# Parallel linear attention and channel MLP: inverse deviations by GpSimd's power, a one-step norm, and another order of loads and transposes in the opening

## The chip, the cores and the metric

One core of one Trainium2 chip runs the kernel. The metric is the device time of one execution in microseconds (us), and the time of a kernel is the median over its runs. Engines are named as the profile names them: PE is TensorE (PEld its weight loads), DVE is VectorE, ACT is ScalarE, POOL is GpSimd, SP is SyncE, which here issues nearly all DMAs.

## The reference

For one batch of S = 2048 rows of D = 640 numbers, with H = 32 heads of 20 and F = 1728 hidden units:

```python
xn = layernorm(x)                          # (x - m) / sqrt(v + 1e-5)
# A: linear attention with learned features
q, k, v = split_heads(xn @ wqkv)
pq, pk = q @ w_phi, k @ w_phi              # per head, 20x20
phi = concat(softmax(p), softmax(-p))      # for q and for k
o = phi_q (phi_k^T v) / (phi_q (phi_k^T 1) + 1e-6)
A = o @ wo
# B: channel MLP; it normalises xn a second time
y = layernorm(xn)
B = gelu(y @ w1 + b1) @ w2 + b2
out = x + A + B
```

Both norms need only the mean m and the variance v of a row of x. The second one is y = (x - m) / sqrt(v (1 + eps) + eps^2), with eps = 1e-5. The attention branch is computed from the same y, with a factor per row (`rs_all`) put back in the exponentials.

## The kernel before, in words

Every float32 operand of a matmul is split into a rounded part `hi` and a rest `lo`, both of a type that PE takes at full rate, and a product is three matmuls: hi by hi, hi by lo, lo by hi (`mm3`, lines 69 to 72). ACT writes `hi` (line 61) and DVE or POOL subtracts to get `lo` (line 64). The work is transposed: channels lie on partitions, and rows of x (tokens) on the free axis, in four blocks of 512 tokens. PE works through the MLP in groups of two chunks of 128 hidden units: a first product (640 channels into 128 units, 5 steps `kc`, 15 matmuls of 512 columns for a chunk), gelu and split of the result, and a second product back to 640 channels (5 output tiles `m`, 6 matmuls each). The order of every engine's instructions in this part is the order in which the program writes them (`manual_schedule`), and each engine takes its queue in order. After the MLP of blocks 0 and 1 come the attention and then the rest of the MLP.

The change is in the opening, which makes block 0's `y` from the rows of x themselves, while the later blocks get theirs from xT (x transposed, in DRAM). It runs so:

- SP loads four tiles of 128 rows (`xb`, tiles 0 to 3; `x0` in the program), the identity for the transposes, the four first chunks of w1 (`r1` of chunks 0 to 3), then tiles 4 to 7 (`x1`), the chunks of w2 (`r2`), block 0 of xT (the MLP's accumulator `acc`), all 320 KB a piece but the identity and xT.
- `stats` (lines 132 to 162) takes mean and variance of each tile on DVE (two `bn_stats`, one `bn_aggr`), scales them into `q`, has ACT take the square roots (line 151; this needs another function table than gelu), and improves the root by a Newton step with reciprocals on DVE, which leaves `ry` (for y) and, some steps later, `rs_all`.
- `centre` (line 166, ACT) subtracts the mean and `scale` (lines 170 and 172, ACT and DVE) multiplies by `ry`.
- `make_y0` (line 179) transposes two tiles on PE into three banks (channel groups c0 of one, c12 and c34 of two chunks of 128 channels), and splits each bank into y's `hi` and `lo`. It is called for tiles 0 and 1 (`y01`, the first half, 256 tokens) and for tiles 2 and 3 (`y23`).
- `half_first` (line 547) runs the first product of chunks 0 and 1 on a half: 30 matmuls of 256 columns. Its results stay in four banks, and their gelu and split (`zs`, four of them: two chunks by two halves) are written into PE's later work.
- PE fills the time before with 18 matmuls of zeros (line 582).
- Then `p10` starts: the first product of chunks 2 and 3 on all 512 tokens of block 0 (two tiles, 30 matmuls; the first of them is the L70 at 18.64 us in the profile), then the second product of chunks 0 and 1 (`p00`), which needs all four `zs`. Beside it runs `next_y` (line 655), which is stepped once per `kc` of the matmuls (a tick): it turns the means and `ry` of tiles 4 to 7 into a row by a small transpose on PE (line 202), copies it (line 204, DVE), sends it to DRAM from ACT's queue (line 207) and back as a broadcast, and makes block 1's `y` from xT with it (lines 681 to 687). The four `zs` are called in it too: the first on the fourth tick, before the row is sent, the others after.

Weights of later chunks are split as they land: `parts[c][0]` is the split of w1's chunk c (line 61 on ACT, line 64 on POOL).

Of the kernel before, what the change touches and what calls it, by code (L numbers as in the profile page):

```python
# [43 lines left out]
DEN_EPS = 1e-6  # L44

# [6 lines left out]
def tile_kernel(ctx: ExitStack, tc: tile.TileContext, x, xT, wkT, wqT, wv, wphi, wo, w1, b1, w2, b2,  # L52
# [30 lines left out]
    cp.tile([P, 56], F32, name="pad")  # L83
    nc.vector.memset(ones1, 1.0)
    nc.scalar.activation(rs_all[0:1, 0:1], ones1[:, 0:1], AF.Sqrt)
# [46 lines left out]
    def stats(ts, xp, xbs, turned=False, eng=nc.vector):  # L132
# [16 lines left out]
        sr = xp.tile([P, 2, n], F32, name="sr", bufs=2)  # L149
        rr = xp.tile([P, 2, n], F32, name="rr", bufs=2)  # L150
# [3 lines left out]
        if turned:  # L154
            nc.vector.scalar_tensor_tensor(sr, sr, -1.0, rr, op0=ALU.mult, op1=ALU.subtract)
        else:
            nc.vector.tensor_tensor(sr, sr, rr, op=ALU.add)
        nc.vector.reciprocal(ry[:, ts], sr[:, 1, :])
        yield
        ra = xp.tile([P, n], F32, name="ra", bufs=2)  # L160
        nc.vector.reciprocal(ra, sr[:, 0, :])
        nc.vector.tensor_tensor(rs_all[:, ts], sr[:, 1, :], ra, op=ALU.mult)

    def centre(t, xb):

        nc.scalar.activation(xb, xb, AF.Identity, bias=mv[:, t, 0:1], scale=-1.0)

    def scale(t, xb, act=False):
        if act:
            nc.scalar.activation(xb, xb, AF.Copy, scale=ry[:, t:t + 1])  # L170
        else:
            nc.vector.tensor_scalar_mul(xb, xb, ry[:, t:t + 1])

    def scale_pair(t):
        scale(t, x0[t])
        scale(t + 1, x0[t + 1][:, :3 * P], True)
        scale(t + 1, x0[t + 1][:, 3 * P:])

    def make_y0(half, xbs, ptile):

        cols = slice(half * 256, half * 256 + 256)
        for c0, n in ((0, 1), (1, 2), (3, 2)):
            ps = ptile()
            for c in range(n):
                for i in range(2):
                    nc.tensor.transpose(ps[:, c * 256 + i * P:c * 256 + (i + 1) * P],
                                        xbs[i][:, (c0 + c) * P:(c0 + c + 1) * P], idt)
            src = ps[:, :n * 256].rearrange("p (c t) -> p c t", c=n)
            cs = slice(c0, c0 + n)
            split(y[0][0][:, cs, cols], y[0][1][:, cs, cols], src)  # L190
            yield
# [27 lines left out]
    class Mlp:  # L219
# [67 lines left out]
        def gelu(self, g, j, pz, gt, hh, hl, out=False):  # L287
# [4 lines left out]
            nc.scalar.activation(gt, pz, AF.Gelu_apprx_tanh, bias=b1t[:, 2 * g + j:2 * g + j + 1])  # L292
            split(hh, hl, gt)

        def passes(self, g, b, ws, hid=None):
# [7 lines left out]
            for j, (w1h, w1l, w2h, w2l) in enumerate(todo):  # L303
# [6 lines left out]
                else:  # L310
# [7 lines left out]
                    nc.scalar.activation(gt[0:64, :], tm, AF.Gelu_apprx_tanh, bias=b1t[0:64, 13:14])  # L318
# [101 lines left out]
        def cross(self, g, bs, before, later):  # L420
# [39 lines left out]
            def gelu(z, i):  # L460
                nc.scalar.activation(z, z, AF.Gelu_apprx_tanh, bias=b1t[:, 2 * g + i:2 * g + i + 1])
# [73 lines left out]
    dmas[0] = mlp.fetch_parts(0, r0)  # L535
    dmas[0][0]()
    x0 += load_x(range(2, 4), xp)
    dmas[1] = mlp.fetch_parts(1, r0)
    dmas[1][0]()
# [7 lines left out]
    def half_first(half, *order):  # L547
# [3 lines left out]
        last = {op[0]: op for op in order}  # L551
        for op in order:
            j, wi, yi, kc = op
            nc.tensor.matmul(pz[j], wc[j][wi][:, kc, :], y[0][yi][:, kc, cols], start=(wi, yi, kc) == (0, 0, 0), stop=last[j] == op)  # L554
# [1118 lines left out]
```

## Time and profile before

| | |
|---|---|
| runs | 703.95, 704.29, 705.25 us; median 704.29 us |
| span of the profiled execution | 702.3 us |
| PE busy | 697.2 us, 99% |
| DVE, POOL, ACT busy | 525.0, 455.9, 365.1 us |
| first real matmul of the opening (L554) | 9.27 us |
| first matmul of full width (L70) | 18.64 us |

The span runs from the first to the last instruction of the profiled execution; the device time holds some 2 us around it. A line of the timeline gives start and duration in us, engine, line of the kernel, operation, what it writes and reads, the shape, and how many instructions of a kind in a row were merged. A line of the groups gives count, busy time and the mean of one in ns. In the queue of SP or ACT (SPq, ACTq) a DMA's line is its issue, not its transfer. A matmul's row starts when PE takes it; its end is modelled, so that matmuls overlap, and the distance of two starts is what one costs.

### The profile page before, as it was taken

The page shows a single profiled execution, that of the slowest core. Times are in us where ns is not written, and L with a number is a line of the kernel's source. Part 1 is how long each engine was busy: PE and PEld are TensorE (multiplying, and loading weights), DVE is VectorE, ACT ScalarE, POOL GpSimd, SP SyncE. Part 2 cuts the span into 40 slices and gives each one's busy share as a digit, 9 for nine tenths or more (in the row PEclk, how much of TensorE's full clock was granted, in tenths as well). Part 3 has the DMA queues.
Part 4 walks back from the last instruction along what each step waited for, and adds up shares of the span by engine and source line. Part 5 has one row for each costly group of instructions (what it writes and reads, how often), then busy time and mean ns, then how long its engine had stood idle before and what let it go on. Part 6 is the DMA issues. An engine that isn't in the chain of part 4 may idle for free.

```text
span 702.3 us, 9854 instructions
## 1 busy us (share of the span) xinstructions
PE 697.2 (99%) x3357; PEld 587.7 (84%) x3357; DVE 525.0 (75%) x856; ACT 365.1 (52%) x615; POOL 455.9 (65%) x388
## 2 busy tenths in 40 slices
PE   9999999999999999999999999999999999999998
PEld 7888888888888888888888888888888888888886
DVE  7868654977755788788888887848688687789783
ACT  6434643344334545454444546457676666659360
POOL 3711314576245997798787969558689997577930
PEclk9999999999999999999999999999999999999999
DMA  9834633485621227325500707884345648872222
GB/s 325 259 110 128 193 108 98 157 279 166 216 106 75 94 76 233 86 91 199 123 1 3 190 0 282 240 241 117 121 145 160 184 148 285 290 274 69 75 76 105
DMA packets 67465, 107.62 MB, mean 153 GB/s; under 512 B 7623, under 2 KB 31975, under 8 KB 65791
## 3 DMA queue, kind: packets, MB, share of 16 engines
q1 hardware_dynamic: 67110, 106.98, 47.7%
q8 instruction: 26, 0.43, 0.3%
q14 instruction: 25, 0.20, 0.1%
q10 hardware_dynamic: 304, 0.01, 0.0%
HBM read 72.42 MB, written 34.55 MB: 152 GB/s over the span
## 4 chain that ended last, share of the span: by engine, by line
PE 98%; DVE 1%; ACT 0%; issue 0%; POOL 0%; DVEq 0%; POOLq 0%
PE bank L910 29%; PE bank L70 19%; PE bank L72 19%; PE bank L71 19%; PE bank L980 3%; PE bank L648 2%; PE bank L1218 1%; PE bank L1219 1%; PE bank L554 1%; PE bank L582 1%; PE bank L313 1%; PE bank L332 1%; PE bank L314 1%; PE bank L333 1%; PE bank L1150 1%; DVE rx L1267 0%
## 5 line engine op out<-in xcount | busy, mean ns | idle before, releaser
L910 PE MATMUL bank<-wkh,y 128*128 128x512 f32 (+1 forms) x480 | 139.5, 364 | 0.0
L70 PE MATMUL bank<-m,w 128*128 128x512 f32 x288 | 113.1, 393 | 0.2 <-ACT w L61 0.2
L64 POOL TENSOR_TENSOR w<-r,w 128x640 fp32r<-128x640 f32 x32 | 52.7, 1659 | 93.4 <-ACT w L61 62.7
L71 PE MATMUL bank<-m,w 128*128 128x512 f32 x288 | 112.1, 389 | 0.0
L72 PE MATMUL bank<-m,w 128*128 128x512 f32 x266 | 103.6, 389 | 0.0
L70 PE MATMUL bank<-y,w 128*128 128x512 f32 (+1 forms) x256 | 99.6, 389 | 0.0
L71 PE MATMUL bank<-y,w 128*128 128x512 f32 (+1 forms) x256 | 98.9, 386 | 0.0
L910 PEld LDWEIGHTS bank<-wkh,y 128*128 128x128 f32 x480 | 87.5, 188 | 13.3
L72 PE MATMUL bank<-y,w 128*128 128x512 f32 (+1 forms) x246 | 95.0, 386 | 0.0
L910 PE MATMUL bank<-wkl,y 128*128 128x512 f32 (+1 forms) x240 | 87.4, 364 | 0.0
L946 ACT ACTIVATE m<-m,rs_all 128x1280 f32<-128x1280 f32 x32 | 43.7, 1365 | 43.5 <-POOL m L945 43.4
L70 PEld LDWEIGHTS bank<-m,w 128*128 128x128 f32 x288 | 54.1, 188 | 11.9 <-ACT w L61 0.6
L71 PEld LDWEIGHTS bank<-m,w 128*128 128x128 f32 x288 | 54.1, 188 | 10.8
L72 PEld LDWEIGHTS bank<-m,w 128*128 128x128 f32 x266 | 49.9, 188 | 10.4
L948 DVE TENSOR_REDUCE sm<-m 128x64 f32<-128x1280 f32 x32 | 47.4, 1482 | 14.9 <-ACT m L946 14.8
L910 PE MATMUL bank<-w,y 128*128 128x512 f32 x240 | 57.4, 391 | 0.0
L945 POOL TENSOR_TENSOR m<-m,mx 128x640 f32<-128x640 f32 (+2 forms) x48 | 44.4, 938 | 19.2 <-DVE mx L934 19.2
L70 PEld LDWEIGHTS bank<-y,w 128*128 128x128 f32 x256 | 48.1, 188 | 10.4 <-ACT bank L1286 0.3
L71 PEld LDWEIGHTS bank<-y,w 128*128 128x128 f32 x256 | 48.1, 188 | 9.5
L337 DVE TENSOR_TENSOR acc<-bank,acc 128x512 f32<-128x512 f32 x70 | 47.1, 683 | 11.8 <-PE bank L72 6.6
L72 PEld LDWEIGHTS bank<-y,w 128*128 128x128 f32 x246 | 46.2, 188 | 9.4
L910 PEld LDWEIGHTS bank<-w,y 128*128 128x128 f32 x240 | 44.4, 188 | 8.5
(236 smaller groups left out, 1544.7 us busy)
## 6 DMA issues: line engine op xcount, KB each, us to landing
r<-in_w SPq DMA_DIRECT2D x52, 320.0 KB
e<-e SPq DMA_DIRECT2D x40, 256.0 KB
e<-acc SPq DMA_DIRECT2D x52, 160.0 KB
t<-t SPq DMA_DIRECT2D x8, 512.0 KB
acc<-in_xT SPq DMA_DIRECT2D x3, 1280.0 KB
tf<-t SPq DMA_DIRECT2D x2, 1536.0 KB
xb<-in_x SPq DMA_DIRECT2D x8, 320.0 KB
t<-in_x SPq DMA_DIRECT2D x8, 320.0 KB
```

Source lines behind the costliest of these rows:

```text
L64: eng.tensor_tensor(lo, src, f(hi), op=ALU.subtract)
L70: nc.tensor.matmul(ps, lh, rh, start=first, stop=False, **kw)
L71: nc.tensor.matmul(ps, lh, rl, start=False, stop=False, **kw)
L72: nc.tensor.matmul(ps, ll, rh, start=False, stop=last, **kw)
L313: nc.tensor.matmul(pz, w1h[:, kc, :], yh[:, kc, :], start=kc == 0, stop=False)
L337: nc.vector.tensor_tensor(acc[b][:, m, :], pw, acc[b][:, m, :], op=ALU.add)
L648: nc.tensor.matmul(ps[:, u * nh * DF:(u + 1) * nh * DF], raw[:nh * DH, u * P:(u + 1) * P], wpt[:nh * DH, g, :nh, 1:], start=True, stop=True)
L910: nc.tensor.matmul(ps, lh[:, kc, c], rh[:, kc], start=n == 0, stop=n == 3 * KC - 1)
L945: subs[n, t] = nc.gpsimd.tensor_tensor(ep[:, s], a, b, op=ALU.subtract)
L946: exps[n, t] = nc.scalar.activation(e, e, AF.Exp, scale=rs_all[:, t:t + 1])
L948: nc.vector.tensor_reduce(sm, e.rearrange("p s (h f) -> p (s h) f", f=DH), axis=AX, op=ALU.add)
L980: nc.tensor.matmul(kvp[g // 2][:, (g % 2) * 240:(g % 2) * 240 + 240].rearrange("p (s f) -> p s f", s=4), v[:, g * VS:(g + 1) * VS], ft[:, ...
```

## The change

- Inverse deviations. `stats` drops the square root on ACT and the Newton step on DVE. POOL now adds a constant to the variance and raises the sum to the power -1/2 (`half[:, 0]` holds -0.5): two POOL instructions for each call. The result lacks a factor (1 + eps)^-0.5, which gelu's `scale=YS` puts back. The calls are now one each for tile 0 and tile 1, one for tiles 2 and 3, one for tiles 4 to 7, one for 8 to 15. `rs_all` is made for all 16 tiles at once later, by five POOL instructions (`deviations`). ACT never loads the table of the square root; the table of gelu is loaded at the start.
- Norm. `centre` and `scale` become one DVE instruction for a tile of 640 columns (`normalise`), with mean and inverse deviation as two operands per row.
- Order. The w1 chunk 1 is loaded ahead of tiles 2 and 3, and chunk 2 ahead of tiles 4 to 7. `make_y0` writes all three `hi` before the first `lo`. The first half's matmuls begin with what needs only `hi`, and the last four of them stand behind the transposes of the second half. The zero matmuls are 13 instead of 18. The statistics of tiles 4 to 7 come after everything of the second half. `next_y` begins two ticks later.

```diff
-    nc.scalar.activation(rs_all[0:1, 0:1], ones1[:, 0:1], AF.Sqrt)
+    nc.scalar.activation(rs_all[0:1, 0:1], ones1[:, 0:1], AF.Gelu_apprx_tanh)
...
-        q = xp.tile([P, 2, n], F32, name="q", bufs=2)
-        eng.tensor_scalar(q[:, 1, :], mv[:, ts, 1], 0.25 * (1 + EPS), 0.25 * EPS * EPS, op0=ALU.mult, op1=ALU.add)
-        eng.tensor_scalar(q[:, 0, :], mv[:, ts, 1], 0.25, 0.25 * EPS, op0=ALU.mult, op1=ALU.add)
+        nc.gpsimd.tensor_scalar_add(ry[:, ts], mv[:, ts, 1], EPS * EPS / (1 + EPS))
+        nc.gpsimd.tensor_tensor(ry[:, ts], ry[:, ts], half[:, 0, :n], op=ALU.pow)
         yield
-        nc.scalar.activation(sr, q, AF.Sqrt)
-        nc.vector.reciprocal(rr, sr)
-        nc.vector.tensor_tensor(rr, rr, q, op=ALU.mult)
...
+    def deviations():
+
+        sq = mtile(6)[:, 0, :16]
+        nc.gpsimd.tensor_scalar_add(rs_all, mv[:, :, 1], EPS)
+        nc.gpsimd.tensor_scalar_add(sq, mv[:, :, 1], EPS * EPS / (1 + EPS))
+        nc.gpsimd.tensor_tensor(rs_all, rs_all, half[:, 0], op=ALU.pow)
+        nc.gpsimd.tensor_tensor(sq, sq, half[:, 1], op=ALU.pow)
+        nc.gpsimd.tensor_tensor(rs_all, rs_all, sq, op=ALU.mult)
+
+    def normalise(t, xb):
+
+        nc.vector.tensor_scalar(xb, xb, mv[:, t, 0:1], ry[:, t:t + 1], op0=ALU.subtract, op1=ALU.mult)
...
-            split(y[0][0][:, cs, cols], y[0][1][:, cs, cols], src)
+            hi, lo = (z[:, c0:c0 + n, cols] for z in y[0])
+            nc.scalar.activation(hi, src, AF.Copy)
+            todo.append((lo, src, hi))
+        yield
+        for lo, src, hi in todo:
+            nc.vector.tensor_tensor(lo, src, f(hi), op=ALU.subtract)
             yield
...
-    for _ in range(18):
+    for _ in range(13):
         nc.tensor.matmul(warm, zero[:, :P], zero, start=True, stop=True)
...
+    finish(s0)
+    finish(s1)
+    for t in range(2):
+        normalise(t, x0[t])
+    for c in range(2):
+        parts[c][0]()
     y01, y23 = make_y0(0, x0[:2], pall), make_y0(1, x0[2:], pall)
+    next(y01)
+    zs = []
+    finish(s23)
+    step(y01, 2)
+    for t in range(2, 4):
+        normalise(t, x0[t])
+    step(y01, 2)
...
+    next(h0)
+    next(y23)
+    finish(h0)
     parts[2][0]()
+    finish(y23)
+    finish(half_first(1, [(j, wi, 0, kc) for kc in range(KC) for j in range(2) for wi in range(2)]
+                      + [(j, 0, 1, kc) for j in range(2) for kc in range(KC)]))
+    finish(s47)
     parts[3][0]()
...
     def next_y():
 
-        for _ in range(3):
+        for _ in range(5):
             yield
         next(rows1)
         zs[0]()
```

What this does to three queues, as their instructions stand in a row. First SP at the program's start, before (`xb` are tiles of x, two, two and four of them; `r_133`, `r_140`, `r_159`, `r_162` the w1 chunks 0 to 3):

```order
L128 DMA xb<-in_x 128x640 x2
L533 DMA idt<-in_ident 128x128
L250 DMA r_133<-in_w 128x640
L128 DMA xb<-in_x 128x640 x2
L250 DMA r_140<-in_w 128x640
L128 DMA xb<-in_x 128x640 x4
L250 DMA r_159<-in_w 128x640
```

And now (`r_136`, `r_139`, `r_154` are chunks 0 to 2):

```order
L132 DMA xb<-in_x 128x640 x2
L524 DMA idt<-in_ident 128x128
L241 DMA r_136<-in_w 128x640
L241 DMA r_139<-in_w 128x640
L132 DMA xb<-in_x 128x640 x2
L241 DMA r_154<-in_w 128x640
L132 DMA xb<-in_x 128x640 x4
```

Tiles 2 and 3 each moved one place back, behind chunk 1, and tiles 4 to 7 two places, behind chunk 2.

Second, DVE from the statistics of tiles 2 and 3 on, before (`y_146` is y's lo, `sr`, `rr`, `q` and `ry` the Newton step):

```order
L138 BN_STATS st<-xb 128x6 x2
L139 BN_AGGR mv<-st 128x2
L138 BN_STATS st<-xb 128x6 x2
L139 BN_AGGR mv<-st 128x2
L64 TENSOR_TENSOR y_146<-bank_231,y_145 128x256
L64 TENSOR_TENSOR y_146<-bank_236,y_145 128x2x256
L64 TENSOR_TENSOR y_146<-bank_243,y_145 128x2x256
L152 RECIPROCAL rr<-sr 128x4
L153 TENSOR_TENSOR rr<-rr,q 128x4
L155 SCALAR_TENSOR_TENSOR sr<-sr,rr 128x4
L158 RECIPROCAL ry<-sr 128x2
L172 TENSOR_SCALAR xb<-xb,ry 128x640
```

And now (`y_149` is y's lo; the first three banks are the first half's, the last three the second's):

```order
L142 BN_STATS st<-xb 128x6 x2
L143 BN_AGGR mv<-st 128x2
L142 BN_STATS st<-xb 128x6 x2
L143 BN_AGGR mv<-st 128x2
L181 TENSOR_TENSOR y_149<-bank_213,y_148 128x256
L181 TENSOR_TENSOR y_149<-bank_217,y_148 128x2x256
L163 TENSOR_SCALAR xb<-xb,mv,ry 128x640 x2
L181 TENSOR_TENSOR y_149<-bank_223,y_148 128x2x256
L181 TENSOR_TENSOR y_149<-bank_271,y_148 128x256
L181 TENSOR_TENSOR y_149<-bank_275,y_148 128x2x256
L181 TENSOR_TENSOR y_149<-bank_281,y_148 128x2x256
L142 BN_STATS st<-xb 128x6 x2
```

The norms of tiles 2 and 3 now stand behind two of the first half's subtractions instead of three and a Newton step, and the statistics of tiles 4 to 7 (the last row is the first of them) behind all of the second half's.

Third, ACT where it takes up the gelus, before (`bank_264`, `bank_265`, `bank_324`, `bank_325` are the four `zs`, the first two of the first half; `bank_391` is the first full tile of `p10`, `r_84` the row for block 1):

```order
L292 ACTIVATE bank_264<-bank_264,b1t 128x256
L61 ACTIVATE m_149<-bank_264 128x256
L207 DMA r_84<-acc_104 8x128
L292 ACTIVATE bank_265<-bank_265,b1t 128x256
L61 ACTIVATE m_150<-bank_265 128x256
L292 ACTIVATE bank_324<-bank_324,b1t 128x256
L61 ACTIVATE m_149<-bank_324 128x256
L292 ACTIVATE bank_325<-bank_325,b1t 128x256
L61 ACTIVATE m_150<-bank_325 128x256
L292 ACTIVATE bank_391<-bank_391,b1t 128x512
```

And now (`bank_359` is the first full tile, `bank_243`, `bank_244`, `bank_296`, `bank_297` the `zs`, `r_87` the row):

```order
L283 ACTIVATE bank_359<-bank_359,b1t 128x512
L62 ACTIVATE m_358<-bank_359 128x512
L283 ACTIVATE bank_243<-bank_243,b1t 128x256
L62 ACTIVATE m_152<-bank_243 128x256
L198 DMA r_87<-acc_107 8x128
L283 ACTIVATE bank_244<-bank_244,b1t 128x256
L62 ACTIVATE m_153<-bank_244 128x256
L283 ACTIVATE bank_296<-bank_296,b1t 128x256
L62 ACTIVATE m_152<-bank_296 128x256
L283 ACTIVATE bank_297<-bank_297,b1t 128x256
```

The gelu and split of the first full tile moved from behind the four `zs` to ahead of them. On DVE the copy of the row (line 204 before) likewise moved behind that tile's subtraction.

More of the change, by code (lines that the diff above doesn't have):

```diff
@@ L82, in tile_kernel @@
     rs_all = cp.tile([P, 16], F32, name="rs_all")
-    cp.tile([P, 56], F32, name="pad")
+    half = cp.tile([P, 2, 16], F32, name="half")
+    cp.tile([P, 24], F32, name="pad")
+    for i in range(2):
+        nc.vector.memset(half[:, i], i - 0.5)
     nc.vector.memset(ones1, 1.0)
-    nc.scalar.activation(rs_all[0:1, 0:1], ones1[:, 0:1], AF.Sqrt)
+    nc.scalar.activation(rs_all[0:1, 0:1], ones1[:, 0:1], AF.Gelu_apprx_tanh)
     e_dram = [tc.dram_tile([2 * D, 512], F32, name=f"e{b}") for b in range(NB)]
@@ L745, in more_stats @@
         yield from stats(range(8, 16), fp, tiles())
-        for _ in range(2):
+        for _ in range(3):
             yield
@@ L762, in prep @@
             yield
+        deviations()
         mr = {2: load_rows(2), 3: load_rows(3, 6)}
```

93 lines of the change are left out of this document (26 added, 67 removed).

## The prediction

> **What bounds the kernel now.** I read the page's shares first, then PE's list of waits, then the chain that ended last in its first 20 us.
>
> ```profile
> span 702.3 us, 9854 instructions
> ...
> PE 697.2 (99%) x3357; PEld 587.7 (84%) x3357; DVE 525.0 (75%) x856; ACT 365.1 (52%) x615; POOL 455.9 (65%) x388
> ```
>
> ```profile
> PE bank L582 <- POOL m L580: 1.3, 1, 1.3
> PE bank L1218 <- DVE acc L1232: 0.2, 1, 0.2
> PE bank L70 <- ACT w L61: 0.2, 1, 0.2
> ```
>
> PE is the bound: it idles 5 us of 702, and the list of its waits for other engines holds 1.7 us. What the change takes off ACT and DVE elsewhere (two table loads beside block 1's work, square roots, Newton steps) can therefore give nothing; only work that PE reaches earlier or later in the opening counts.
>
> ```profile
> 1.31 7.12 PE bank L582 x18
> 9.77 4.16 PE bank L554 x29
> 13.93 1.09 PE bank L186 x10
> 15.02 3.79 PE bank L554 x30
> ```
>
> ```profile
> 18.64 0.40 PE L70 MATMUL bank<-y,w 128*128 128x512 f32 x1
> ...
> 25.62 0.39 PE L70 MATMUL bank<-m,w 128*128 128x512 f32 x1
> ...
> 26.76 0.39 PE L72 MATMUL bank<-m,w 128*128 128x512 f32 x1
> ...
> 44.03 0.39 PE L71 MATMUL bank<-y,w 128*128 128x512 f32 x1
> ```
>
> The chain is PE alone: 18 zero matmuls, first half's matmuls, ten transposes for the second half, its matmuls, then full width from S = 18.64 us on. The row at 25.62 is the first matmul of `p00`'s second product, 26.76 its sixth, 44.03 the place in block 1 where PE needs the last `lo` of y. Five starts lie between 25.62 and 26.76, so a matmul of full width costs 0.228 us. From 26.76 on PE runs without a wait worth naming, so I take the start of that sixth matmul as the measure: its shift is the change of the time. At 25.62 PE came 6.98 us after S, which is 30 matmuls and a small transpose: it did not wait for the hidden units.
>
> **When the second half can be transposed.** SP issues a load only when the one eight places before it has landed, so its issues tell the landings.
>
> ```profile
> 7.76 0.33 SPq L250 DMA_DIRECT2D r<-in_w  x1
> 8.93 0.33 SPq L251 DMA_DIRECT2D r<-in_w  x1
> ...
> 9.73 0.33 SPq L251 DMA_DIRECT2D r<-in_w  x1
> ```
>
> These mark tile 2 (7.7 us), tile 3 (8.9) and w1's chunk 1 (9.7). The three have one size and now come in the order chunk 1, tile 2, tile 3. So chunk 1 lands at 7.7, tile 2 at 8.9, tile 3 at 9.7: the new order costs the tiles about a microsecond.
>
> ```profile
> 7.98 0.88 DVE L138 BATCH_NORM_STATS2 st<-xb 128x6 f32<-128x320 f32 x2
> 8.89 0.21 DVE L139 BATCH_NORM_AGGREGATE mv<-st 128x2 f32<-128x12 f32 x1
> 9.02 0.83 DVE L138 BATCH_NORM_STATS2 st<-xb 128x6 f32<-128x320 f32 x2
> 9.88 0.21 DVE L139 BATCH_NORM_AGGREGATE mv<-st 128x2 f32<-128x12 f32 x1
> 10.01 1.57 DVE L64 TENSOR_TENSOR y<-bank,y 128x256 fp32r<-128x256 f32 x3
> ```
>
> DVE takes 1.04 us from one tile's statistics to the next (7.98 to 9.02), and 1.07 from the second's start to its end. From 9.0 us that gives tile 3's variance at 11.1. Before, it was there at 10.1. Then stand two of the first half's three subtractions; all three took 1.57, two of them (one narrow, one wide) about 0.9, so DVE is free at 12.0.
>
> ```profile
> L172 DVE TENSOR_SCALAR xb<-xb,ry 128x640 f32<-128x640 f32 x2 | 1.1, 554 | 0.1
> ...
> L1001 POOL TENSOR_TENSOR m<-m,w 128x40 f32<-128x40 f32 x16 | 15.7, 983 | 0.0
> ...
> L999 POOL TENSOR_TENSOR w<-sm,w 128x2 f32<-128x2 f32 x16 | 3.1, 195 | 0.0
> ```
>
> The norm with two operands per row is not in the trace; its bounds are the 0.55 of the same instruction with one operand and the 0.9 of a pass of two statistics over a tile. I take 0.55, the same operation. Two norms, overlapping by 0.1, end at 12.9. POOL's power isn't in the trace either. Its bounds are the 0.2 of a two-element and the 0.98 of a 40-element operation with two inputs; I take 0.2, the shape it has. Then add and power after the variance end at 11.6, before DVE is free at 12.0. Up to a power of 0.4 us DVE's subtractions hide it; beyond that each tenth counts.
>
> So the transposes of tile 3 start at 12.95 instead of at 13.9: 0.9 gained. PE is there in time. ACT splits chunk 1 (landed at 7.7, 0.7 us) ahead of the first y, so the first half's matmuls start near 8.9 instead of 9.27. The first 26 at 0.12 us, with a wait for y's `lo` until 12.0 before the last five, end at 12.6. Then come nine transposes at 0.11, the four matmuls left over (0.5), which cover the split of the new banks, and 30 at 0.12 (15.02 to 18.64). S = 12.95 + 1.0 + 0.5 + 3.6 = 18.0 us, 0.6 earlier. The first half's transposes themselves come near 7.1 instead of 8.3, since 13 zero matmuls end before 7 and the norms of tiles 0 and 1 at about 7.05, but this gain is lost again at the join.
>
> **Who waits for ACT's new order.** ACT's full-width gelu now stands ahead of the four `zs`, and it waits for PE.
>
> ```profile
> 22.07 0.53 ACTq L207 DMA_DIRECT2D r<-acc  x1
> 22.64 0.45 ACT L292 ACTIVATE bank<-bank,b1t 128x256 f32<-128x256 f32 x1 [0.47 <-DVE m L64]
> ...
> 24.16 0.45 ACT L292 ACTIVATE bank<-bank,b1t 128x256 f32<-128x256 f32 x1
> 24.64 0.38 ACT L61 ACTIVATE m<-bank 128x256 fp32r<-128x256 f32 x1
> 24.92 0.66 ACT L292 ACTIVATE bank<-bank,b1t 128x512 f32<-128x512 f32 x1
> 25.61 0.60 ACT L61 ACTIVATE m<-bank 128x512 fp32r<-128x512 f32 x1
> 26.11 0.66 ACT L292 ACTIVATE bank<-bank,b1t 128x512 f32<-128x512 f32 x1
> ```
>
> ```profile
> 21.76 0.27 DVE L204 COPY acc<-bank 8x128 f32<-8x128 f32 x1
> ...
> 25.05 0.42 DVE L64 TENSOR_TENSOR m<-bank,m 128x256 fp32r<-128x256 f32 x1 [0.33 <-ACT m L61]
> ...
> 26.57 0.68 DVE L64 TENSOR_TENSOR m<-bank,m 128x512 fp32r<-128x512 f32 x1
> ```
>
> Call G the start of that gelu. It follows the 15th matmul: S + 14 x 0.228 + 0.4 = S + 3.6. The wide `hi` starts at G + 0.69 and ends at G + 1.29, and the first z's gelu starts at G + 1.19 (24.92, 25.61, 26.11). The next instruction on ACT is the row's DMA. It waits for the copy on DVE, which now stands behind the wide subtraction: G + 1.3 + 0.7 + 0.2 = G + 2.2. The issue holds ACT for 0.57 (22.07 to 22.64), so the second z starts at G + 2.8, and with 0.76 a z (24.16 to 24.92) the third at G + 3.6 and the fourth at G + 4.4. A z's `hi` ends 0.86 after its start (0.48 + 0.38), its `lo` 1.31 after (24.16 to 25.47). PE's `p00` needs the third z's `hi` for its first matmul, G + 4.5 = S + 8.1, and the fourth's `lo` for its fifth, G + 5.75 = S + 9.35. The sixth starts at S + 9.6. Before, it started at S + 8.1.
>
> With S = 18.0 that is 27.6 or 27.7 us instead of 26.76: the 0.6 gained turn into 0.9 lost. Other claims end earlier: POOL's split of chunk 3, now behind the power for tiles 4 to 7, whose statistics end at about 19.8 (four tiles at 1.04 behind the second half's last subtraction near 15.6), is done at 21.8, just when PE takes it.
>
> **What else moves.** The row for block 1 leaves 1.8 us later (G + 2.25 = 23.9 instead of 22.07), and its multiplications begin one accumulation later on DVE.
>
> ```profile
> 42.87 0.67 DVE L687 TENSOR_TENSOR y<-xb,y 128x512 fp32r<-128x512 f32 x1
> ```
>
> This is the last `lo` of block 1's y, done at 43.5 for the matmul at 44.03. Following DVE's queue from the last accumulation of `p00` (33.6) through fourteen operations at 0.6 to 1.1 us, I get 45.05 for it now, and PE wants it at 44.03 + 0.9: a wait of 0.1, at most 0.5.
>
> ```profile
> 114.01 1.56 POOL L64 TENSOR_TENSOR w<-r,w 128x640 fp32r<-128x640 f32 x1 [16.96 <-ACT w L61]
> ```
>
> `deviations` falls into 17 us in which POOL has nothing to do: free, unless five small operations took that long. The power for tiles 8 to 15 likewise stands, between two weight splits of POOL, in an idle stretch of 8 us:
>
> ```profile
> 83.20 1.57 POOL L64 TENSOR_TENSOR w<-r,w 128x640 fp32r<-128x640 f32 x1 [8.48 <-ACT w L61]
> ```
>
> The factor in gelu and the memsets of `half` cost nothing that PE sees.
>
> The sum is -0.6 + 1.5 + 0.1 = +1.0 us on the profiled span, 703.3. The median of the runs lies 2.0 above the span, so I say 705.3 us. The runs shown differ among themselves by 1.3, and 0.2%, which is 1.4 us, is about what a measurement of this kernel can tell from no change.
>
> **Rivals.**
>
> GpSimd late (slower). For it: the inverse deviations now stand on POOL's queue ahead of all norms, and the two prices that matter, the power's and POOL's readiness, are not in the trace. With a power of 0.98, tile 3's norm ends at 13.45, S is 18.55, and the time 705.9. And POOL's first computation after its opening memset came late for other reasons:
>
> ```profile
> 8.63 1.56 POOL L64 TENSOR_TENSOR w<-r,w 128x640 fp32r<-128x640 f32 x1 [7.38 <-ACT w L61]
> ```
>
> An ISA row (a configuration) stands ahead of it in POOL's queue; now it stands ahead of the first add at 5.0. If POOL were ready only at 8.6, the first norms would end at 10.2, tile 3's variance would come at 12.2, PE would start the first half at 11.2, S would be 19.6 and the time 706.9. It decides once the first norms end after 8.9. Against it: the gap of 7.38 ended with ACT, so POOL may have been ready long before. The Trainium skill, GPSIMD Engine Reference, "Instruction dispatch", says that the first call of a freshly loaded kernel pays about 6 us after the configuration; by an estimate from it, counted from where that gap begins (8.63 - 7.38), POOL would be ready near 7.2, S 18.3 and the time 705.6; the trace shows nothing against it, since POOL was not wanted before 8.6. Chance of this rival with a result beyond 0.2%: 0.34.
>
> The hidden units in time (no change). If ACT's order did not hold PE, the sixth matmul would come at S + 8.1 = 26.1, 0.6 earlier: 703.7. For it: the banks that the `zs` read are all computed before S. Against it: the queue's order and the DMA's wait on DVE, both fixed. Chance 0.13.
>
> The opening without its joins (faster). If the tiles landed as early as before and the `zs` were no wait, PE would run from 8.9 without a stop: 60 matmuls at 0.12 and ten transposes, S = 17.1, 1.5 earlier, 702.8. It needs both my waits to be wrong: 0.07.
>
> **The numbers.** The forecast has 0.44, with the rival of the hidden units 0.57 for a time within 0.2%. Slower by more: 0.36, the late GpSimd and 0.02 for other mishaps. Faster by more: 0.07. The range goes from the hidden units in time, 703.6, to POOL ready only at 8.6 with some margin, 707.1; the forecast's own range, from the norm's upper bound and y's wait, is 704.9 to 705.7.
>
> **What would show it.** In the profile of the changed kernel (lines by its own numbers): the second half's transposes at 13.0 us; the first full-width L71 at 18.0; ACT's first `zs` gelu behind the full-width one at about 22.8, then an issue of the row's DMA at 23.9 after an idle wait on DVE; the first matmul of the second product at 26.2 and the sixth at 27.7; L149 on POOL at 0.2 us each. I am wrong if POOL's first add starts well after 5.0 us, if L149 takes more than 0.4 us, or if PE reaches the second product's sixth matmul before 26.8 or after 28.2.

## The result and the profile after

| | before | after |
|---|---|---|
| median of the runs | 704.12 us (5 runs, 703.94 to 705.25) | 707.77 us (5 runs, 707.27 to 709.09) |
| span of the profiled execution | 702.3 us | 706.0 us |
| first matmul of full width | 18.64 us | 18.46 us |
| sixth matmul of the second product | 26.76 us | 28.52 us |

The ratio of after to before is 1.0052, with a 95% interval of 1.0041 to 1.0063: slower by 3.7 us, where I had forecast 1.0 and given 707.1 us as the upper end. Executions that ran at a lower granted clock or far longer than the rest (the first profiled one of the split below, at a clock of 0.753, that of the load order with the copy, at 0.852, one of the three edits with the copy, at 1421 us, and one of the kernel before, at 997 us) are left out of every ratio, and no time is read from those two profiles. PE's list of waits, which held nothing over 0.2 us besides the memset, now reads:

```profile
PE bank L575 <- POOL m L573: 1.3, 1, 1.3
PE bank L173 <- DVE xb L163: 1.0, 1, 1.0
PE bank L72 <- DVE y L681: 0.7, 2, 0.5
PE bank L73 <- POOL w L65: 0.6, 1, 0.6
PE bank L71 <- ACT m L62: 0.5, 1, 0.5
PE bank L1210 <- DVE acc L1224: 0.2, 1, 0.2
```

The second row lies in the opening; the next three are new, and each falls behind the first matmul of full width. PE's timeline shows where (the L73 at 23.11 is the second full tile's third matmul, 26.95 the first of the second product, 45.79 and 46.99 lie in block 1):

```profile
7.88 1.20 PE L173 MATMUL bank<-idt,xb 128*128 128x128 f32 x9 [1.02 <-DVE xb L163]
9.23 3.73 PE L545 MATMUL bank<-y,w 128*128 128x256 f32 x26
...
18.46 0.40 PE L71 MATMUL bank<-y,w 128*128 128x512 f32 x1
...
23.11 0.50 PE L73 MATMUL bank<-y,w 128*128 128x512 f32 x1 [0.61 <-POOL w L65]
...
26.95 0.50 PE L71 MATMUL bank<-m,w 128*128 128x512 f32 x1 [0.46 <-ACT m L62]
...
28.52 0.40 PE L73 MATMUL bank<-m,w 128*128 128x512 f32 x1
...
45.79 0.50 PE L72 MATMUL bank<-y,w 128*128 128x512 f32 x1 [0.47 <-DVE y L681]
...
46.99 0.50 PE L72 MATMUL bank<-y,w 128*128 128x512 f32 x1 [0.24 <-DVE y L681]
```

Taking the same matmul in both traces, after is 0.18 us ahead at 18.46 and behind everywhere later: by 0.58 once chunk 3's lo is there (23.47 against 22.89), by 1.33 at 26.95, by 1.76 at 28.52, by 3.08 behind block 1's y (48.02 against 44.94), and by 3.71 at the end. So the loss is -0.18, +0.76 (chunk 3), +1.18 (hidden units), +1.32 (block 1's y) and +0.63 in small gaps that lie at 192 and 462 us in the kernel before (194 and 465 us in the changed one), of which the chain gives the last to a DMA's landing.

POOL in the opening shows the price that was not in the trace before, and what stands behind it:

```profile
4.93 0.23 POOL L148 TENSOR_SCALAR ry<-mv 128x1 f32<-128x1 f32 x1 [3.67 <-DVE mv L143]
5.24 0.58 POOL L149 TENSOR_TENSOR ry<-ry,half 128x1 f32<-128x1 f32 x1
5.92 0.59 POOL L148 TENSOR_SCALAR ry<-mv 128x1 f32<-128x1 f32 x1
...
11.40 0.72 POOL L149 TENSOR_TENSOR ry<-ry,half 128x2 f32<-128x2 f32 x1
...
20.17 0.24 POOL L148 TENSOR_SCALAR ry<-mv 128x4 f32<-128x4 f32 x1 [2.66 <-DVE mv L143]
20.49 1.05 POOL L149 TENSOR_TENSOR ry<-ry,half 128x4 f32<-128x4 f32 x1
21.50 1.55 POOL L65 TENSOR_TENSOR w<-r,w 128x640 fp32r<-128x640 f32 x1
```

The power takes 0.58 us for one element per partition, 0.72 for two, 1.05 for four. The second addition (5.92) took 0.59 us where the first took 0.23: it began 0.06 us behind DVE's first norm (5.86, 0.61 long) and ended with it, which made the second norm late too. The last row is chunk 3's lo, done at 23.05, which PE wanted at 22.34. DVE beside it:

```profile
20.11 0.17 DVE L189 COPY sc<-mv 128x4 f32<-128x4 f32 x1
21.57 1.51 DVE L189 COPY sc<-ry 128x4 f32<-128x4 f32 x1 [1.29 <-POOL ry L149]
23.00 0.88 DVE L64 CAST w<-r 128x640 fp32r<-128x640 f32 x2
23.80 0.68 DVE L65 TENSOR_TENSOR m<-bank,m 128x512 fp32r<-128x512 f32 x1
24.40 0.27 DVE L195 COPY acc<-bank 8x128 f32<-8x128 f32 x1
```

One copy of 128x4 takes 0.17 us and the next, of the same shape, 1.51: it began 0.07 us behind POOL's subtraction and ended with it (23.08 and 23.05). ACT's row DMA and the second of the zs (25.28; the third follows at 26.04) then stand in the order that the prediction told:

```profile
22.08 0.66 ACT L283 ACTIVATE bank<-bank,b1t 128x512 f32<-128x512 f32 x1 [5.60 <-PE bank L73]
...
24.70 0.53 ACTq L198 DMA_DIRECT2D r<-acc  x1
25.28 0.45 ACT L283 ACTIVATE bank<-bank,b1t 128x256 f32<-128x256 f32 x1 [1.09 <-DVE m L65]
```

### The profile page after: what moved, and what is told of

Its sections match the earlier page's. It is cut to its first block, busy times and chain, and to the rows that moved or that the text cites. A ratio compares the mean times of both kernels' runs of the same rounds, so it can differ in the third digit from the quotient of the medians.

```text
span 706.0 us, 9818 instructions
## 1 busy us (share of the span) xinstructions
PE 697.7 (99%) x3352; PEld 585.6 (83%) x3352; DVE 522.6 (74%) x828; ACT 356.7 (51%) x602; POOL 468.3 (66%) x401
## 4 chain that ended last, share of the span: by engine, by line
PE 82%; DVE 7%; POOL 4%; issue 2%; DMA 2%; ACT 1%; SPq 1%; ACTq 0%; POOLq 0%; DVEq 0%
PE bank L902 23%; PE bank L71 17%; PE bank L72 17%; PE bank L73 17%; PE bank L972 2%; POOL m L937 2%; PE bank L642 1%; PE bank L1210 1%; PE bank L1211 1%; DMA xb<-in_x 1%; POOL m L948 1%; DVE st L142 1%; DVE xb L677 1%; SPq L1005 1%; PE bank L323 1%
## 5 line engine op out<-in xcount | busy, mean ns | idle before, releaser
L71 PE MATMUL bank<-m,w 128*128 128x512 f32 x288 | 113.4, 394 | 0.6 <-ACT m L62 0.5
L73 PE MATMUL bank<-m,w 128*128 128x512 f32 x266 | 103.6, 389 | 0.0
L71 PE MATMUL bank<-y,w 128*128 128x512 f32 (+1 forms) x256 | 99.6, 389 | 0.0
L73 PE MATMUL bank<-y,w 128*128 128x512 f32 (+1 forms) x246 | 95.1, 386 | 0.6 <-POOL w L65 0.6
L71 PEld LDWEIGHTS bank<-m,w 128*128 128x128 f32 x288 | 54.1, 188 | 12.9 <-ACT m L62 0.9
L73 PEld LDWEIGHTS bank<-m,w 128*128 128x128 f32 x266 | 49.9, 188 | 10.5
L71 PEld LDWEIGHTS bank<-y,w 128*128 128x128 f32 x256 | 48.1, 188 | 10.4 <-ACT bank L1278 0.3
L73 PEld LDWEIGHTS bank<-y,w 128*128 128x128 f32 x246 | 46.2, 188 | 10.4 <-POOL w L65 1.0
L1204 POOL TENSOR_TENSOR e<-e,m 128x512 fp32r<-128x512 f32 x28 | 41.3, 1475 | 15.4 <-ACT m L1203 14.6
```

The source lines that it names most:

```text
L71: nc.tensor.matmul(ps, lh, rh, start=first, stop=False, **kw)
L73: nc.tensor.matmul(ps, ll, rh, start=False, stop=last, **kw)
L1204: mlp.after(1, lambda: nc.gpsimd.tensor_tensor(pl, e, f(ph), op=ALU.subtract))
```

## The experiments

Theory A: the loss comes from places in the queues (POOL's split of chunk 3 behind the power, ACT's full-width gelu and the row's DMA ahead of the zs, the row two ticks later). Theory B: it comes from the power's price. Theory C came up with the first runs: DVE and POOL hold each other up when a copy or a norm meets a subtraction, and small shifts decide whether they meet (the expectations call it a race, or collisions, for the port). Ratios are to the kernel before, run on the same chip, with 95% intervals.

### The split first

```diff
-    finish(s47)
     parts[3][0]()
+    finish(s47)
```

> Chunk 3's split stands ahead of the statistics of tiles 4 to 7 on POOL, everything else as in the changed kernel. Order of the hidden units (theory A: what costs is that ACT takes the full-width gelu, then waits with the row's DMA, ahead of the other three zs): the wait of 0.6 us in the second full tile goes and the copy of ry (1.51 us beside POOL's subtraction) falls to 0.2, but the third z still starts at about 25.7, so the sixth matmul of the second product only moves from 28.5 to 28.1, block 1's y still comes late, and the time is about 707.2, 0.5 below the changed kernel. POOL's queue (theory B: the power ahead of that split is what costs): both waits come from it, the sixth matmul comes at 26.6 to 26.9, and the time falls by 2.5 or more, to 705.2 or less.

Measured: 1.0040 (1.0027 to 1.0054), 0.12% or 0.8 us below the changed kernel's ratio, with intervals that overlap. As theory A had it; theory B's 2.5 us are excluded. Since no time is read from its profile, the edit was run again, together with the one-element copy on POOL that is told below:

> Chunk 3's split first, with the copy that takes the race out; to be read against the changed kernel with that copy alone (708.2). Theory A: no wait for chunk 3, ry's copy on DVE 0.2 us, but the full-width gelu still stands ahead of the zs and the row: sixth matmul of the second product at 28.1, a wait for block 1's y of about 1 us, time 707.3 to 707.8. Theory B (POOL's queue): 706 or less.

Measured: 1.0038 (1.0026 to 1.0050), against 1.0046 with that copy alone, with intervals that overlap. PE's waits in it:

```profile
PE bank L71 <- ACT m L62: 1.0, 1, 1.0
PE bank L72 <- DVE y L682: 0.6, 2, 0.4
```

Chunk 3's wait of 0.6 is gone, and the wait for the hidden units grew from 0.5 to 1.0: they were the next thing late. The split is worth little as long as the zs stand where they stand.

### The hidden units early

```diff
+    for z in zs:
+        z()
     rows1 = rows(1, 1, xp, Banks(7), 1, nc.scalar)
...
         next(rows1)
-        zs[0]()
         finish(rows1)
...
-        for z in zs[1:]:
-            z()
```

> All four zs are written straight after chunk 3's split, ahead of the first full-width tile; POOL's queue is as in the changed kernel. Theory A: ACT has 5.6 idle us there (16.5 to 22.1), so the hidden units are ready before PE wants them; what is left is the 0.6 us wait for chunk 3's lo. Second product's first matmul at 26.2 and its sixth at 27.35 instead of 28.5; block 1's y waits less, 0 to 0.6; time 705.0 to 706.0. Theory B: the zs were held by the stretched copy behind POOL, not by their place; the time falls by less than 0.7, to 707.1 or more.

Measured: 1.0049 (1.0036 to 1.0062), no gain, as theory B had it; but the trace tells another reason. DVE, then POOL, then PE's waits:

```profile
5.97 0.61 DVE L163 TENSOR_SCALAR xb<-xb,mv,ry 128x640 f32<-128x640 f32 x1
7.32 1.85 DVE L163 TENSOR_SCALAR xb<-xb,mv,ry 128x640 f32<-128x640 f32 x1 [0.73 <-POOL ry L149]
```

```profile
7.28 3.29 POOL L65 TENSOR_TENSOR w<-r,w 128x640 fp32r<-128x640 f32 x2
```

```profile
PE bank L173 <- DVE xb L163: 2.3, 1, 2.3
...
PE bank L72 <- DVE y L680: 1.1, 2, 0.8
PE bank L73 <- POOL w L65: 0.6, 1, 0.6
```

The wait of L71 for ACT's hidden units is gone, as theory A said: from 25.13 to 46 us the distance to the kernel before stays at 2.2 to 2.4. But block 1's y, whose row still left late, now costs 1.65 (2.36 to 4.01) instead of 1.32. And in this execution the second norm took 1.85 us instead of 0.61, so that the first full-width matmul came at 20.11: chunk 0's hi was done at 7.21 here and at 7.75 in the changed kernel's profile, and so POOL's subtraction started 0.04 us ahead of the norm (7.28 and 7.32) instead of at its end (7.82). This is theory C's race.

### No power

```diff
-        nc.gpsimd.tensor_tensor(ry[:, ts], ry[:, ts], half[:, 0, :n], op=ALU.pow)
+        nc.gpsimd.tensor_tensor(ry[:, ts], ry[:, ts], half[:, 0, :n], op=ALU.mult)
```

This kernel leaves the power out and so does not compute the norm; it serves for the time alone.

> The power is replaced by a product of the same shape and operands, so that the norms are scaled wrongly; this leaves the power out of the time. It should take some 0.2 us instead of 0.6 to 1.05. Theory B (the power's price): chunk 3's lo is done at 22.2 and PE doesn't wait for it, the first norms come 0.7 earlier, and the time falls by 2 or more, to 705.7 or less. Theory A (the order): the opening gains 0.1 to 0.3, the wait for chunk 3 goes (0.6), the zs stand where they stood, sixth matmul at 27.8 to 28.0, and time 706.7 to 707.1.

Measured: 1.0026 (1.0016 to 1.0036), median 706.33, between what the theories expected. The product took 0.19 us where the power had 0.72 for two elements, and the first full-width matmul came at 17.41 instead of 18.46. Some of that is not the power's: tile 2's statistics started at 8.15 instead of 8.87, a landing that varies from run to run (8.33 in the run with the row early). Chunk 3's wait went; a wait of 1.0 for the hidden units and 1.1 us at block 1's y were left. The copy of ry was as long as with the power:

```profile
10.72 0.19 POOL L149 TENSOR_TENSOR ry<-ry,half 128x2 f32<-128x2 f32 x1
```

```profile
19.69 1.51 DVE L189 COPY sc<-ry 128x4 f32<-128x4 f32 x1 [0.44 <-POOL ry L149]
```

So the stretched copy comes of its place beside POOL's subtraction. The power's price makes some of the loss, and the places the rest; how much each makes can't be read off this run, since the opening also had the earlier landing.

### Three edits, and the two that suffice

The first kernel has the split first, the zs early as above, and `next_y` one tick earlier; the second only the split and the tick, by which the row and the zs come ahead of the full-width gelu:

```diff
     def next_y():
-        for _ in range(5):
+        for _ in range(4):
             yield
```

> Three edits at once: chunk 3's split ahead of the statistics of tiles 4 to 7, the four zs straight after them, and the row for block 1 one tick earlier, so that it leaves ahead of the full-width gelu. Theory A: no wait is left from 18.5 us on, sixth matmul at 26.6, the row's DMA near 22.3, block 1's y as in the kernel before; time 703.9, as the kernel before or 0.2 below it. Theory B, if the power's price in the opening still tells: above 705.

Measured: 1.0009 (1.0000 to 1.0018).

> Two edits: chunk 3's split ahead of the statistics of tiles 4 to 7, and the row for block 1 (with the zs that follow it) one tick earlier, on the last step of the first full-width tile and so ahead of its gelu on ACT. Theory A (the places of the split, the row and the zs make the loss): no wait for chunk 3, the row's DMA at 22.4, third z's gelu at 23.7, no wait for the hidden units or block 1's y, and the time is within 0.8 of the kernel before, 704.0 to 705.2 (with some runs 1.2 longer where the norm meets POOL's subtraction). Theory B (the power's price in the opening makes it): 706 or more.

Measured: 1.0011 (1.0001 to 1.0020), median 704.98, runs from 703.93 to 707.53. ACT in this kernel:

```profile
22.59 0.53 ACTq L198 DMA_DIRECT2D r<-acc  x1
23.17 0.45 ACT L283 ACTIVATE bank<-bank,b1t 128x256 f32<-128x256 f32 x1 [6.10 <-DVE m L65]
23.93 0.45 ACT L283 ACTIVATE bank<-bank,b1t 128x256 f32<-128x256 f32 x1
```

The row leaves at 22.59 instead of 24.70, ry's copy (21.40) takes 0.17 us, and PE's list holds no wait over 0.2 us behind the opening. Two lines of order take back four fifths of the loss with the power in place: theory A.

### The row early alone

> The changed kernel with the row and the zs one tick earlier and nothing else (the other half of the kernel of two edits). Theory A with the port: ry's copy still ends at 23.1 behind POOL's subtraction, so PE now waits 1.2 us for it after the 15th matmul instead of 0.6 for chunk 3; the hidden units are in time; block 1's y is still about a microsecond late; time 706.3 to 707.2. Rival (the two edits are worth what they are worth each by itself; together they took 2.8, the split alone 0.4): 705.5 or less.

Measured: 1.0042 (1.0028 to 1.0057), median 707.13, runs from 705.55 to 709.02. In its profile (span 704.4) PE waits 1.1 us for ry's copy, which again took 1.50 beside POOL's subtraction, and not at all for block 1's y; my theory's late y was wrong here:

```profile
PE bank L193 <- DVE sc L189: 1.1, 1, 1.1
```

Half of the repair leaves a wait at the same time, for another operand.

### The stretched copy by itself

```diff
...
+            if b == 1 and a == 1:
+                nc.scalar.activation(sc[:, :, a, :], src, AF.Copy)
...
```

> The changed kernel with the copy of ry into the row's tile (1.51 us on DVE beside POOL's subtraction) on ACT instead, which is idle there. Theory A (places): the copy takes 0.2 us, DVE's casts and the row's copy come 0.4 earlier, the sixth matmul of the second product at 28.1 instead of 28.5, and the time 707.3 to 707.6, since chunk 3's wait and the place of the zs remain. Rival (the stretched copy alone is what holds DVE, and with it everything): the time falls by the 1.3 us that it was stretched, or more, to 706.5 or less.

Measured: 1.0044 (1.0032 to 1.0056), median 707.14. Not the 1.3 us of the rival; the gain of about half a microsecond is the size that theory A had, but the interval takes in no gain. Its profiled execution (708.94 us, the longest of the five) had the second norm at 1.81 us.

### The race for the port

```diff
+    nc.gpsimd.tensor_copy(rs_all[:, 0:1], x0[1][:, 0:1])
     for c in range(2):
         parts[c][0]()
```

The copy reads one element of the normed tile 1, so that POOL cannot begin chunk 0's subtraction ahead of DVE's norm.

> A one-element copy on POOL that reads the normed tile 1 stands ahead of chunk 0's split, so that POOL's subtraction cannot start before DVE's second norm is done; the rest is the changed kernel. Theory C (a race for the port: when chunk 0 lands early, POOL's subtraction starts first and the norm takes 1.85 instead of 0.61 us, as in the profile of the hidden units written early): the norm takes 0.6 in every run, the runs above 708.5 disappear, the median is 707.3 to 707.7 and the spread under 0.8. Rival (the spread is the DMAs' landing alone): still 707.2 to 709.1.

Measured: 1.0046 (1.0033 to 1.0058), runs from 707.71 to 708.44. The spread shrank from 1.8 to 0.7 us, as theory C had it; the loss hardly shrank: the median (708.22) is 3.5 us above the kernel before on the same chip, against 3.65 for the changed kernel. In the changed kernel's own profile the norm had not met POOL (0.61 us), so the copy had nothing to save in such a run; besides, the gap near 462 us was 1.0 us long in this profile against 0.4. Which of the two kept the median up is not shown.

The same copy in the kernel of three edits:

> The kernel of three edits (chunk 3's split first, the four zs early, the row one tick earlier) with the one-element copy that holds POOL's first subtraction behind the second norm. Theory C: its runs, which went from 704.2 to 706.3 without the copy, lie between 704.0 and 704.9, median 704.3, no difference from the kernel before. Rival (landing alone): median 705.1 as without it.

Measured: 1.0004 (0.9995 to 1.0013), no difference from the kernel before; eight of the ten runs counted lie between 704.5 and 705.4, the others at 705.6 and 706.1. Against 1.0009 without the copy the intervals overlap, and the runs reach beyond the 704.9 that theory C had given, so what the copy adds in this kernel is not shown.

### The arithmetic alone, in the order of before

> The kernel before with the new arithmetic alone: GpSimd's power, the norm in one DVE operation, the factor in gelu, the deviations at once; loads, matmuls, zs, row and zero matmuls stand in the order of before. Theory A: the arithmetic isn't what costs; the norms of tiles 2 and 3 end at about 12.8 instead of 13.8, the first full-width matmul comes at 17.7 to 18.6, and the time is 703.2 to 704.6, with runs 1.2 longer where the second norm meets POOL's subtraction (theory C). Theory B: power on POOL ahead of the norms costs 1 us or more in this order too, 705.5 or more.

Measured: 1.0018 (1.0010 to 1.0027), median 706.36, slower, which theory A alone had not expected. DVE and POOL in its opening:

```profile
7.06 2.42 DVE L165 TENSOR_SCALAR xb<-xb,mv,ry 128x640 f32<-128x640 f32 x2 [1.16 <-POOL ry L149]
...
12.91 2.13 DVE L165 TENSOR_SCALAR xb<-xb,mv,ry 128x640 f32<-128x640 f32 x2
```

```profile
7.07 1.55 POOL L65 TENSOR_TENSOR w<-r,w 128x640 fp32r<-128x640 f32 x1
...
12.60 1.57 POOL L65 TENSOR_TENSOR w<-r,w 128x640 fp32r<-128x640 f32 x1
```

Both pairs of norms met a subtraction and took 2.42 and 2.13 us instead of 1.14. The power is part of the cause in a new way: POOL frees itself at the very moment at which DVE may start the norm. With the one-element copy ahead of chunk 0's subtraction:

> The new arithmetic in the order of before, with the one-element copy on POOL that holds chunk 0's subtraction behind the second norm. Theory C (the port's collisions are what that arithmetic costs, 2.42 us for the first pair of norms instead of 1.13): the first pair takes 1.15, PE's first transposes end 1.2 earlier; the norms of tiles 2 and 3 still can meet chunk 1's subtraction; time 704.6 to 705.6. Rival (the power itself costs): 706.2 or more, as without the copy.

```profile
7.07 1.14 DVE L165 TENSOR_SCALAR xb<-xb,mv,ry 128x640 f32<-128x640 f32 x2 [1.16 <-POOL ry L149]
...
11.64 2.14 DVE L165 TENSOR_SCALAR xb<-xb,mv,ry 128x640 f32<-128x640 f32 x2
```

Measured: 0.9996 (0.9988 to 1.0005), median 704.09, runs from 703.99 to 704.78. The copy of one element takes the whole loss away, 2.3 us between the medians (0.2 of it is the kernel before, which was faster by that in this series). The power costs nothing on balance here: the first full-width matmul comes at 18.64 as before. With the second pair taken from DVE as well, onto ACT (the other edits of this run are told in its expectation):

```diff
...
-        normalise(t, x0[t])
+        nc.scalar.activation(x0[t], x0[t], AF.Identity, bias=nb[:, t - 2:t - 1], scale=ry[:, t:t + 1])
...
```

> The new arithmetic in the order of before with the first pair of norms free of the port (as h3_arithmetic_gate), and the norms of tiles 2 and 3 on ACT, which is idle there and shares no port with POOL (scale ry, bias minus m times ry, made by one small DVE and one small POOL operation); the first half's last five matmuls stand behind the second transposes, since chunk 1's lo comes at 13.2. Theory C (only the port stood in the way): second norms done at 13.2 instead of 13.8, first full-width matmul at 18.3 instead of 18.6, time 703.6 to 704.0, at most 0.1% under the kernel before. Rival (PE's own work bounds the opening, or the later lo holds it): 704.1 to 704.6, no gain over the copy alone.

Measured: 1.0001 (0.9992 to 1.0010), no further gain. The second norms were done at 13.37, but PE was not ready for them:

```profile
9.18 4.50 PE L544 MATMUL bank<-y,w 128*128 128x256 f32 x25
13.52 1.25 PE L174 MATMUL bank<-idt,xb 128*128 128x128 f32 x10
14.53 4.43 PE L544 MATMUL bank<-y,w 128*128 128x256 f32 x35
18.80 0.40 PE L71 MATMUL bank<-y,w 128*128 128x512 f32 x1
```

So the rival held: behind a start at 9.2 PE's own first half and its operands fill the time, and neither version beats the kernel before by what can be measured.

### The load order

```diff
-    for c in range(2):
-        dmas[c] = mlp.fetch_parts(c, r0)
-        dmas[c][0]()
+    dmas[0] = mlp.fetch_parts(0, r0)
+    dmas[0][0]()
     x0 += load_x(range(2, 4), xp)
+    dmas[1] = mlp.fetch_parts(1, r0)
+    dmas[1][0]()
```

Chunk 2 likewise goes behind tiles 4 to 7 (the change had moved these by one place, from the eighth to eleventh load to the ninth to twelfth, not by two); the base is the kernel of two edits.

> The kernel of two edits with the loads in the order of before (tiles 2 and 3 ahead of chunk 1, tiles 4 to 7 ahead of chunk 2). By the prediction's step (the new order costs the tiles about a microsecond) the statistics of tile 2 start at 7.9 instead of 8.7, and if nothing else bounds the opening the first full-width matmul comes at 17.6 and the time falls to 704.3. Rival (chunk 1 is wanted as early as the tiles): its hi comes at 10.6, the first half's matmuls wait for it on PE, the first full-width matmul comes at 18.3 to 18.9 and the time is 705.0 to 705.8.

Measured: 1.0029 (1.0018 to 1.0039), above the 1.0011 of its base; its profiled execution had the second norm at 1.81 us. With the race taken out:

> The kernel of two edits, with the loads in the order of before and with the copy that holds POOL's first subtraction behind the second norm, so that it is read against the kernel of two edits without the race (704.0 to 705.0). If the new load order costs the tiles a microsecond and nothing else bounds the opening: tile 2's statistics at 8.0, first full-width matmul near 17.6, time 703.6 to 704.2. Rival (chunk 1's hi bounds the first half): hi at about 10.0, first half's matmuls held on PE, first full-width matmul at 18.2 to 18.8, time 704.6 to 705.4.

Measured: 1.0041 (1.0028 to 1.0054), beyond even the rival. ACT in its opening, read for the order alone:

```profile
10.05 0.74 ACT L62 ACTIVATE w<-r 128x640 fp32r<-128x640 f32 x1 [1.72 <-DMA r<-in_w]
10.81 1.36 ACT L177 ACTIVATE y<-bank 128x256 fp32r<-128x256 f32 x3
```

ACT's queue has chunk 1's hi ahead of y's three, so that the late chunk holds y too, and PE's longest wait in that profile ends with ACT's y. The new load order thus goes with the new order of ACT: undone by itself, it gave no gain in either run (1.0029 and 1.0041 against 1.0011).

## Why the prediction was wrong, point by point

The forecast sum was +1.0 us and the measured one +3.71. Of the 2.7 us between them 0.46 arose in the opening, 0.46 between S and the sixth matmul, 1.22 at block 1's y and 0.63 in the small gaps. Three steps failed: the power's price, taken as that of any two-input operation; DVE and POOL holding each other up, for which the sum had no term; and the start of block 1's y on DVE, taken some 0.6 us too early. Two of the signs that the prediction had named for being wrong appeared: L149 took 0.58 to 1.05 us, over 0.4, and the sixth matmul came at 28.52, after 28.2.

- **PE as the bound, the sixth matmul as the measure.** The bound was right. The measure was not: it moved by 1.76 us, the time by 3.71, since PE did wait behind it.
- **The opening, S = 18.0.** It was 18.46. The step that failed is the power at 0.2 us, "the shape it has": 0.72 for two elements, so that ry for tiles 2 and 3 came at 12.12 and DVE, free at 11.9, waited 0.28; the norms took 0.61, not 0.55. (By the prediction's own times DVE hid a power of up to 0.6 us, not 0.4: 11.6 with 0.2, and DVE free at 12.0. Measured, it was 0.45, from the power's start at 11.40 to 11.88.) The tile 3 transposes came at 13.34, not 12.95. Tile 2's landing (8.87) and the first half's start (9.23 against 8.9) were near.
- **Chunk 3's split, "done at 21.8, just when PE takes it".** It was done at 23.05: the statistics ended at 20.08 instead of 19.8, and add and power took 1.4 instead of 0.4. Wait: 0.6, net cost 0.76 at that place. The sum had nothing for it; but the hidden units would have held PE anyway, as the second run of the split shows (their wait grew to 1.0), so it is part of the 10.06 of the next point and not a loss on top.
- **ACT's order, +1.5 from S to the sixth matmul.** The mechanism was right: from S it took 10.06 us, 9.6 forecast, 8.1 before. The 0.46 on top come from DVE, which the forecast let run free: the copy of 1.51 us kept its casts until 23.88, so the row's copy came at 24.40 and the DMA at 24.70, where S + 5.85 had been forecast (24.3 with the S measured).
- **Block 1's y, "a wait of 0.1, at most 0.5".** Two waits, by which the distance grew by 1.32, the largest term missed. DVE's queue started it at 35.10 instead of 33.6, behind `p00`'s last accumulation. The 33.6 was too early by the prediction's own numbers: it is when that accumulation ended in the kernel before, behind a multiplication (DVE's next row starts at 33.62). Without the multiplication, at the distance of 1.36 between those before it (29.91, 31.27), it would end at 33.3, and 0.9 later is 34.2. The rest of the lateness, 0.9, is that of the two waits before. And two of its operations ran beside POOL's subtractions for the same y (32.58 to 39.78) for 1.83 and 1.76 us where the sum had at most 1.1, though one of the kernel before, at 34.66, had taken 1.78:

```profile
35.10 1.83 DVE L677 TENSOR_TENSOR xb<-xb,m 128x512 f32<-128x512 f32 x1
...
38.57 1.76 DVE L681 TENSOR_TENSOR y<-xb,y 128x512 fp32r<-128x512 f32 x1
...
42.66 0.67 DVE L677 TENSOR_TENSOR xb<-xb,m 128x512 f32<-128x512 f32 x1
```

  The runs show that it hangs on the row: with the zs early and the row late the wait stays, with the row early it goes.
- **The deviations and the power for tiles 8 to 15, free.** Right, though dearer than thought: five operations took 6.65 us on POOL (100.23 to 106.88), two of them 2.9 each, and PE waited for none.
- **Rivals.** GpSimd late was right on the side of the price (its 0.98 is close to the 1.05 for four elements), and wrong on its place: it priced the norms, not what stood behind the power in POOL's queue. That its S of 18.55 lies near the measured 18.46 is in part luck, since for two elements the power took 0.72. POOL was ready at once: the first add ran at 4.93, 0.09 us behind the variance. The Trainium skill's page GPSIMD Engine Reference, "Instruction dispatch", has about 6 us for the first call behind a configuration; POOL's configuration stood at 1.20, by which the first addition would have run near 7.2, and it ran at 4.93, so the trace does not agree. The hidden units were not in time: PE waited 0.5 us for them, and the sixth matmul came at S + 10.06, not S + 8.1. The opening without its joins did not come about either (S = 17.1 against 18.46).
- **What the prediction left unused.** Before's own trace held the sign. In it a DVE operation of 128x4, L153, takes 0.74 us at 11.77 where the same one takes 0.16 at 6.65, and ends with POOL's subtraction (12.51 and 12.49):

```profile
11.77 0.74 DVE L153 TENSOR_TENSOR rr<-rr,q 128x4 f32<-128x4 f32 x1
```

```profile
10.91 1.58 POOL L64 TENSOR_TENSOR w<-r,w 128x640 fp32r<-128x640 f32 x1 [0.19 <-ACT w L61]
```

What stays open: the 0.63 us at 192 and 462 us, which most of the kernels show in sizes from 0.1 to 1.0 us, and of which only the second was followed to a DMA; why the copy on POOL by itself did not lower the median; and how the loss divides between the power's price and the places.

## What to carry to other kernels

When an operation moves to a queue whose price for it no row shows, follow everything that stands behind it in that queue, not only its own consumer: here a weight split came 1.2 us later than forecast, and a copy behind the power met that split and took 1.51 us instead of 0.17. In this kernel with one busy engine a removed wait uncovered the next one at nearly the same time, so repair the places together before judging any of them. And where DVE copies or scales an SBUF tile at the moment POOL becomes free, order the two by a dependence; a race decided by 0.04 us cost 1.2 here.

## What the hardware showed

- GpSimd's power grows with the elements per partition: 0.58 us for 1, 0.72 for 2, 1.05 for 4, 1.67 for 8, 2.93 for 16, about 0.43 plus 0.155 for each. A product of the same shapes took 0.19 for 1 and for 2, 0.20 for 4.
- DVE's norm of 128x640 takes 0.61 us alone and 1.81 to 1.85 when POOL's subtraction started first; the copy of 128x4 0.17 and 1.51. It goes the other way too: POOL's addition of 128x1 took 0.23 us alone and 0.59 when DVE's norm started 0.06 us ahead of it. The Trainium skill, SBUF — State Buffer, "Who interferes with whom", says that copies, casts and `tensor_scalar` between SBUF tiles can hold a port pair that DVE and GpSimd share, and that whichever issues first keeps it for the whole instruction. The trace agrees: the norm of 1.85 us ended at 9.17, some 0.3 behind POOL's first subtraction (7.28, and 1.54 long). The same section has operations with at most one SBUF input outside those modes free of it; `bn_stats` beside POOL's second subtraction took 0.87 us for two, as alone.
